# Attention and a gated feed-forward block on one core: contraction in pieces of 128 rows whose halves exchange column blocks, and a start on half of the first rows

## The chip, the cores and the metric

The kernel runs on one core of a Trainium2 chip. The metric is the device time of one execution in microseconds (us). Five engines run their own instruction streams and meet at semaphores: PE (TensorE; PEld is its weight load, which runs beside matmuls), DVE (VectorE), ACT (ScalarE), POOL (GpSimd) and SP (SyncE, which here only issues DMAs). PE writes its sums into PSUM, eight banks of 128 x 512 f32 numbers; ACT and DVE take them out into SBUF.

## What is computed

```python
xn = layernorm(x)                               # x: 2048 x 448, bf16
q  = (xn @ wq)                                  # 16 heads of 256
p  = softmax(q @ k.T * 256 ** -0.5)             # the last 512 cached keys; 8 key heads, each used by two
s  = concat(p @ v) @ wo
g  = silu((gelu(xn @ w_gate) * (xn @ w_up)) @ w_down)   # 1792 hidden columns
out = x + s * g
```

The contraction of the first products runs over D = 448 = 7 x 64 = 3 x 128 + 64 numbers. That remainder of 64 is what the change is about.

## The kernel before

A small recorder (`Rec.op`, L65) takes every operation in program order with the tiles that it reads and writes; each engine then executes its own list in that order, and the recorder derives the semaphore waits. So the order of the calls in the program is the order on each engine.

The 2048 rows are worked in NQC = 4 chunks of QC = 512 rows, each of TPC = 4 tiles of 128 rows.

**Start.** SP issues four DMAs for the tiles of chunk 0, then the gate and up weights in four slices (`load_gu`), chunk 1's rows after the second slice, then w_down and the other rows. PE spins on zeros (`warm(12)`, L308). DVE computes the statistics of the four tiles (`ln_stats`, L293), ACT the square roots for two tiles at a time (L335), DVE normalises (`ln_norm`, L299), PE transposes each tile in 14 pieces (`ln_tr`, L321), and ACT or DVE copies the 128 x 896 result into `xnT` (L327, L329).

**Layout.** `xnT` holds the transposed rows in NK = 7 pieces of 64, each stored twice: on partitions 0 to 63 and again on 64 to 127. The gate weights lie on partitions 0 to 63 and the up weights on 64 to 127 of one tile `wgu`; `wq` holds the even head of a pair below and the odd head above. A matmul of 64 rows uses half of PE, so two run side by side, a "pair": the lower half of the array makes the gate column block in one bank, the upper half the up block in the next.

**Feed-forward stage, `gate_up` (L367).** For each chunk, 14 blocks f of 7 pairs. Block n takes the banks 2(n mod 3) and the next one. ACT applies gelu to the gate bank (L379, 128x512), DVE multiplies the up bank by it (L381, 128x512) into `actT`. While this runs, `ln_later` and `ln_later2` prepare the next chunk: statistics on DVE, 1/std on POOL, two normalised copies on DVE (L299 twice), and a DMA transposition on SP's queue (L241) into `xnT`. After the 14 blocks come four `down` products (L387) for the chunk's tiles; those of the last chunk are spread over the attention's first slots (`fill`).

**Queries, `q_burst` (L407).** Four heads at once, later eight: per block 7 pairs into two banks (alternating 0-1 and 2-3; in the first burst 4-5, 0-1, 2-3, 0-1), and one ACT copy of 128x1024 (L422).

**Attention.** 64 heads-by-chunk, four slots of 128 rows each: `scores` (L433, banks 4 and 5 in turn, exponential on ACT L437, reciprocal and scaling on DVE L439 and L440, DMA transposition on SP), `values` (L453, copied out by DVE L459), and the output product `outproj` (L473). The last tiles end on DVE (L482, L484) and four output DMAs.

POOL's queue carries the wq, V and wo pieces (`load_piece`), one after each of certain blocks.

Of the kernel before, what the change touches and what calls it, by code (L numbers as in the profile page):

```python
# [22 lines left out]
class Rec:  # L23
# [41 lines left out]
    def op(self, eng, fn, r=(), w=(), dma=False, after=(), lane=None):  # L65
# [17 lines left out]
        for d, raw in deps:  # L83
            if d.eng == eng and not d.dma and not dma and (eng == "tensor" or not raw and eng != "gpsimd"):
                continue
            d.inc = d.waited = True
            o.deps.append(d)
# [54 lines left out]
def bass_recurrent_scan__sliding_block_cached__geglu_ffn__prompt_kernel(nc, A_x, A_k, A_v, A_wq, A_wo, B_x, B_wg, B_wu, B_wd, out):  # L142
# [6 lines left out]
    QC, TPC, HP = 512, 4, 64  # L149
    NQC = S // QC  # L150
    NT = NQC * TPC
    NK = D // HP
    NF, NJ, NE = F // P, W // P, Dh // P
    assert S % QC == 0 and D % HP == 0 and NE == 2 and NJ == 4 and Hq == 2 * Hkv and Hq % 4 == 0 and NF % 2 == 0
# [4 lines left out]
    with es:  # L159
# [20 lines left out]
        xnT, _ = sb("xnT", [P, NQC, NK, QC], BF16)  # L180
# [3 lines left out]
        wq, _ = sb("wq", [P, NK, Hkv, Dh], BF16)  # L184
        wo, _ = sb("wo", [P, Hq * NE, D], BF16)
        gu_at = off[0]
        wgu, x_at = sb("wgu", [P, NK, F], BF16)
        x4, _ = sb("x4", [P, NT, D], BF16)
        NX = 4
        xn2, d_at = sb("xn2", [P, NX, NK, 2, HP], BF16)  # L190
        wd, _ = sb("wd", [P, NF, D], BF16)
        actT, hb_at = sb("actT", [P, NF, QC], BF16)
        NHB = 4
        hb, ffn_end = sb("hb", [P, NHB, QC], BF16)

# [11 lines left out]
        def fill_pr(at, end):  # L207
            while at + 2 * W <= end:
                t_, at = sb("pr%d" % len(pr), [P, W], BF16, at)
                pr.append(t_)  # L210
# [33 lines left out]
        dve(lambda e: e.memset(actT[:, NF - 1, :], 0.0), w=[("actT", NF - 1)])  # L244
# [9 lines left out]
        wg_v = B_wg.rearrange("(k p) f -> p k f", p=HP)  # L254
        wu_v = B_wu.rearrange("(k p) f -> p k f", p=HP)
        cuts = [0, 2, 6, 10, NF]
        fslice = {f: s for s in range(4) for f in range(cuts[s], cuts[s + 1])}

        def load_gu(s):
            a, b = cuts[s] * P, cuts[s + 1] * P  # L260
            dma("sync", wgu[0:HP, :, a:b], wg_v[:, :, a:b], w=[("wgu", 0, s)])
            dma("sync", wgu[HP:P, :, a:b], wu_v[:, :, a:b], w=[("wgu", 1, s)])
# [5 lines left out]
        act(lambda e: e.activation(small[:, 2:3], small[:, 0:1], ACT.Sqrt), r=[("eps",)], w=[("warm",)])  # L268
        for sl in range(4):
            load_gu(sl)  # L270
            if sl == 1:
                load_x(1)
        dma("sync", wd[:, :, :], B_wd.rearrange("(f p) d -> p f d", p=P), w=[("wd",)])
        for c in range(2, NQC):
# [5 lines left out]
        wq_v = A_wq.rearrange("(k p) (g two m) -> p k g two m", p=HP, two=2, m=Dh)  # L280
        pieces = [(wq[lo * HP:(lo + 1) * HP, k, :, :], wq_v[:, k, :, lo, :], ("wq", lo, k))
                  for k in range(NK) for lo in range(2)]
# [13 lines left out]
        def ln_norm(t, copies=2):  # L296
            s = t % NX
            for o in range(copies):
                dve(lambda e, o=o: e.tensor_scalar(  # L299
                    xn2[:, s, :, o, :], x4[:, t, :].rearrange("p (k d) -> p k d", k=NK), mv[:, t, 0:1],  # L300
                    rstd[:, t:t + 1], op0=ALU.subtract, op1=ALU.mult),
                    r=[("x4", t), ("mv", t), ("rstd", t)], w=[("xn2", s, o)])

        def warm(n):

            def run(e):
                for _ in range(n):
                    ins = e.matmul(bank(3), lhsT=actT[:, NF - 1, 0:P], rhs=actT[:, NF - 1, :], start=True, stop=True)  # L308
                return ins
            pe(run, r=[("actT", NF - 1)], w=[("ps", 3)])  # L310

        def ln_tr(t):
            parts = ((act, 4),), ((dve, 5),), ((act, 6),), ((dve, 7),)
            parts = [(eng, b, 0, NK) for eng, b in parts[t]]
            for eng, b, a, z in parts:
                tp = bank(b).bitcast(BF16)

                def tr(e, tp=tp, a=a, z=z):
                    for k in range(a, z):
                        for lo in (0, HP):  # L320
                            ins = e.transpose(tp[lo:lo + HP, (k - a) * P:(k - a + 1) * P], xn2[:, t, k, 0, :], ident[:, :])  # L321
                    return ins
                pe(tr, r=[("xn2", t, 0), ("ident",)], w=[("ps", b)])
                dst = xnT[:, 0, a:z, t * P:(t + 1) * P]
                src = tp[:, 0:(z - a) * P].rearrange("p (k q) -> p k q", q=P)
                if eng is act:
                    act(lambda e, dst=dst, src=src: e.activation(dst, src, ACT.Copy), r=[("ps", b)], w=[("xnT", 0, t, a)])  # L327
                else:
                    dve(lambda e, dst=dst, src=src: e.tensor_copy(dst, src), r=[("ps", b)], w=[("xnT", 0, t, a)])  # L329

        for t in range(TPC):
            ln_stats(t)
            if t % 2:
                a, b = t - 1, t + 1
                act(lambda e, a=a, b=b: e.activation(std[:, a:b], mv[:, a:b, 1], ACT.Sqrt, bias=small[:, 0:1]),  # L335
                    r=[("mv", a), ("mv", t), ("eps",)], w=[("std", a)])
        for a in range(0, TPC, 2):
            dve(lambda e, a=a: e.reciprocal(rstd[:, a:a + 2], std[:, a:a + 2]),  # L338
                r=[("std", a)], w=[("rstd", a), ("rstd", a + 1)])
            ln_norm(a, 1)  # L340
            ln_norm(a + 1, 1)
        warm(12)
        for t in range(TPC):
            ln_tr(t)
        xn0 = [("xnT", 0, t, 0) for t in range(TPC)]
# [9 lines left out]
        def ln_later2(t):  # L355
            c, t4 = divmod(t, TPC)
            ln_norm(t)
            dmaT(xnT[:, c, :, t4 * P:(t4 + 1) * P], xn2[:, t % NX, :, :, :].rearrange("p k a d -> p (k a d)"),
                 r=[("xn2", t % NX, 0), ("xn2", t % NX, 1)], w=[("xnT", c, t4)])

        def xn(c):
            return [("xnT", c, t) for t in range(TPC)] if c else xn0
# [4 lines left out]
        def gate_up(c, f):  # L367

            n = c * NF + f
            s = 2 * (n % NGB)  # L370

            def run(e):
                for k in range(NK):
                    for b, lo in ((s, 0), (s + 1, HP)):
                        ins = e.matmul(bank(b), lhsT=wgu[lo:lo + HP, k, f * P:(f + 1) * P],  # L375
                                       rhs=xnT[lo:lo + HP, c, k, :], start=k == 0, stop=k == NK - 1)
                return ins
            pe(run, r=xn(c) + [("wgu", 0, fslice[f]), ("wgu", 1, fslice[f])], w=[("ps", s), ("ps", s + 1)])
            act(lambda e: e.activation(hb[:, n % NHB, :], bank(s), ACT.Gelu_apprx_tanh),  # L379
                r=[("ps", s)], w=[("hb", n % NHB)])  # L380
            dve(lambda e: e.tensor_tensor(actT[:, f, :], bank(s + 1), hb[:, n % NHB, :], ALU.mult),  # L381
                r=[("ps", s + 1), ("hb", n % NHB)], w=[("actT", f)])

        def down(c, t, part=range(NF)):
            b = (6, 7, 7, 2)[t] if c == NQC - 1 else 6 + t % 2
# [21 lines left out]
        def q_burst(i0, heads):  # L407

            c, h0 = divmod(i0, Hq)
            for n in range(heads):  # L410
                hp, e_ = divmod(n, 2)
                s = 2 * (n % 2) if i0 else (4, 0, 2, 0)[n]
                buf, name, _ = q_slot(i0 + 2 * hp)

                def run(e, hp=hp, e_=e_, s=s):
                    for k in range(NK):
                        for b, lo in ((s, 0), (s + 1, HP)):
                            ins = e.matmul(bank(b), lhsT=wq[lo:lo + HP, k, h0 // 2 + hp, e_ * P:(e_ + 1) * P],  # L418
                                           rhs=xnT[lo:lo + HP, c, k, :], start=k == 0, stop=k == NK - 1)
                    return ins  # L420
                pe(run, r=xn(c) + [("wq", lo, k) for lo in range(2) for k in range(NK)], w=[("ps", s), ("ps", s + 1)])
                act(lambda e, e_=e_, s=s, buf=buf: e.activation(  # L422
                    buf[:, :, e_, :], psum[:, s * 512:(s + 2) * 512].rearrange("p (a q) -> p a q", a=2), ACT.Copy),
                    r=[("ps", s), ("ps", s + 1)], w=[(name, e_)])
# [94 lines left out]
        for c in range(NQC):  # L519
            lead = 4 if c == 0 else 1  # L520
            for f in range(NF):
                gate_up(c, f)
                if c + 1 < NQC and lead <= f < lead + 2 * TPC:
                    t, half = divmod(f - lead, 2)
                    (ln_later2 if half else ln_later)((c + 1) * TPC + t)
# [15 lines left out]
        for d, slots in ((0, range(0, 4)), (1, range(4, 12)), (2, range(16, 20)), (3, range(20, 24))):  # L541
# [4 lines left out]
        for i in range(NI):  # L546
            for t in range(TPC):
                scores(i, t)
                if 4 * i + t in fill:
# [53 lines left out]
```

## Time and profile before

| | us |
|---|---|
| median of 3 runs (558.99 to 559.34) | 559.27 |
| the execution that the profile shows | 558.75 |
| its span, first to last instruction | 557.0 |
| PE busy in the span | 548.7 |
| DVE, ACT, POOL busy | 324.1, 296.3, 89.7 |
| first `gate_up` matmul starts at | 9.28 |
| `gate_up`, one chunk (196 matmuls) | 21.3 |
| `down`, one chunk (56 matmuls) | 10.7 |
| `q_burst` of four heads, of eight | 6.0, 12.2 |

Times inside the execution are counted from the span's start. In a timeline line the first number is the start, the second the time from the group's first start to its last end, then engine, line of the kernel, operation, what it writes and reads, shape and count; in brackets stands the engine's idle time before it and what ended it. A matmul's shown duration includes its passage through the array, so consecutive ones overlap: the rate is read from start to start.

### The profile page before, as it was taken

What the parts mean: (1) busy time and instruction counts of PE and PEld (TensorE: products, weight loads), DVE (VectorE), ACT (ScalarE), POOL (GpSimd) and SP (SyncE); (2) the same over time, 40 slices, a digit from 0 to 9 for tenths busy, and PEclk for the clock granted to TensorE, in tenths of its full rate; (3) what the DMA queues carried; (4) which work ended last, traced back from release to release, by engine and by line L of the source; (5) the groups of instructions that cost most, each with busy time, mean ns of one, the idle gap of its engine ahead of it and who ended that gap; (6) DMA issues with size and microseconds to landing.
All of it is one profiled execution on the core that took longest, in us unless ns stands there. A gap on an engine that the chain in (4) does not pass through costs nothing.

```text
span 557.0 us, 9857 instructions
## 1 busy us (share of the span) xinstructions
PE 548.7 (99%) x3498; PEld 258.8 (46%) x3532; DVE 324.1 (58%) x835; ACT 296.3 (53%) x673; POOL 89.7 (16%) x125
## 2 busy tenths in 40 slices
PE   8999999999999999999999999999999999999997
PEld 4544444444444444444444444444444444444445
DVE  5727446143462688078728744782688078638774
ACT  4423233247746665655575656556665655565631
POOL 0232323200000121001411110042121002411123
PEclk9999999999999999999999999999999999999999
DMA  8996846932453365245535542445354254634552
GB/s 196 276 177 102 138 102 143 264 110 70 95 87 67 67 96 98 46 94 104 112 81 95 104 86 44 100 92 137 75 96 100 34 95 97 120 88 98 93 95 52
DMA packets 169552, 58.83 MB, mean 106 GB/s; under 512 B 160160, under 2 KB 166432, under 8 KB 169504
## 3 DMA queue, kind: packets, MB, share of 16 engines
q1 hardware_dynamic: 166208, 45.50, 44.3%
q0 software_dynamic: 3152, 12.65, 8.7%
q8 instruction: 28, 0.46, 0.4%
q14 instruction: 20, 0.16, 0.1%
q10 hardware_dynamic: 144, 0.06, 0.0%
HBM read 17.92 MB, written 1.84 MB: 35 GB/s over the span
## 4 chain that ended last, share of the span: by engine, by line
PE 97%; DVE 2%; issue 1%; DMA 0%; ACT 0%
PE ps L453 20%; PE ps L433 20%; PE ps L418 18%; PE ps L473 17%; PE ps L375 15%; PE ps L387 8%; DVE tmp L482 0%; DVE xr L484 0%; DVE stats L293 0%; DMA x<-in_A_x_dram 0%; PE ps L321 0%; ACT xnT L327 0%; DVE mv L294 0%; DVE xn L299 0%; DVE rstd L338 0%
## 5 line engine op out<-in xcount | busy, mean ns | idle before, releaser
L437 ACT ACTIVATE pr<-ps 128x512 bf16<-128x512 f32 x256 | 152.7, 597 | 121.4 <-PE ps L433 117.9
L433 PE MATMUL ps<-kT,qT 128*128 128x512 bf16 x493 | 147.7, 379 | 2.0 <-issue 1.4
L453 PE MATMUL ps<-pT,V 128*128 128x512 bf16 x497 | 129.1, 379 | 0.8
L439 DVE RECIPROCAL rden<-den 128x1 f32<-128x1 f32 x256 | 41.5, 162 | 148.2 <-ACT pr L437 129.8
L473 PE MATMUL ps<-wo,oT 128*128 128x448 bf16 (+1 forms) x536 | 116.2, 344 | 0.0
L440 DVE TENSOR_SCALAR pr<-pr,rden 128x512 bf16<-128x512 bf16 x256 | 108.0, 422 | 9.0
L418 PE MATMUL ps<-xnT,wq 64*128 64x512 bf16 x896 | 98.3, 376 | 0.0
L422 ACT ACTIVATE qT<-ps 128x1024 bf16<-128x1024 f32 x64 | 65.5, 1023 | 40.6 <-PE ps L418 40.6
L375 PE MATMUL ps<-xnT,wgu 64*128 64x512 bf16 x784 | 85.3, 376 | 0.8 <-ACT xnT L327 0.8
L459 DVE CAST oT<-ps 128x512 bf16<-128x512 f32 x124 | 84.5, 682 | 0.7 <-PE ps L453 0.5
L453 PEld LDWEIGHTS ps<-pT,V 128*128 128x128 bf16 x512 | 50.0, 98 | 60.2 <-issue 0.3
L473 PEld LDWEIGHTS ps<-wo,oT 128*128 128x128 bf16 x536 | 52.4, 98 | 51.0
L433 PEld LDWEIGHTS ps<-kT,qT 128*128 128x128 bf16 x512 | 49.1, 98 | 55.8 <-issue 4.5
L381 DVE TENSOR_TENSOR actT<-ps,hb 128x512 bf16<-128x512 f32 x56 | 38.1, 685 | 57.2 <-ACT hb L379 55.3
L418 PEld LDWEIGHTS ps<-xnT,wq 64*128 64x128 bf16 x896 | 43.0, 94 | 54.6 <-DVE acc L494 2.5
L379 ACT ACTIVATE hb<-ps 128x512 bf16<-128x512 f32 x56 | 33.4, 597 | 51.4 <-PE ps L375 51.4
L375 PEld LDWEIGHTS ps<-xnT,wgu 64*128 64x128 bf16 x784 | 39.4, 94 | 46.0 <-issue 1.6
L437 ACT ACTIVATION_READ_ACCUMULATOR pr<-ps 128x1 f32 x256 | 49.8, 195 | 0.0
L387 PE MATMUL ps<-wd,actT 128*128 128x448 bf16 x224 | 46.2, 353 | 0.1
L498 POOL TENSOR_TENSOR tmp<-acc,gy 128x448 f32<-128x448 f32 x16 | 16.5, 1034 | 158.6 <-DVE acc L494 158.6
L513 POOL TENSOR_SCALAR tmp<-tmp 128x448 f32<-128x448 f32 x16 | 9.0, 563 | 187.8 <-ACT tmp L512 187.8
L387 PEld LDWEIGHTS ps<-wd,actT 128*128 128x128 bf16 x224 | 21.7, 98 | 22.2 <-issue 1.3
(43 smaller groups left out, 172.4 us busy)
## 6 DMA issues: line engine op xcount, KB each, us to landing
pT<-pr SPq DMA_TRANSPOSE x256, 2.4
wq<-in_A_wq_dram POOLq DMA_DIRECT2D x14, 256.0 KB, 5.2
wo<-in_A_wo_dram POOLq DMA_DIRECT2D x4, 896.0 KB, 6.6
V<-in_A_v_cache_dram POOLq DMA_DIRECT2D x4, 512.0 KB, 5.0
xr<-in_A_x_dram POOLq DMA_DIRECT2D x4, 448.0 KB, 3.9
wd<-in_B_w_down_dram SPq DMA_DIRECT2D x1, 1568.0 KB, 18.5
wgu<-in_B_w_gate_dram SPq DMA_DIRECT2D x3, 448.0 KB, 9.5
wgu<-in_B_w_up_dram SPq DMA_DIRECT2D x3, 448.0 KB, 11.1
```

Of the source, the lines that this page charges most:

```text
L375: ins = e.matmul(bank(b), lhsT=wgu[lo:lo + HP, k, f * P:(f + 1) * P], rhs=xnT[lo:lo + HP, c, k, :], start=k == 0, stop=k == NK - 1)
L381: dve(lambda e: e.tensor_tensor(actT[:, f, :], bank(s + 1), hb[:, n % NHB, :], ALU.mult), r=[("ps", s + 1), ("hb", n % NHB)], w=[("actT", f)])
L387: pe(lambda e, f=f: e.matmul(bank(b, D), lhsT=actT[:, f, t * P:(t + 1) * P], rhs=wd[:, f, :], start=f == 0, stop=f == NF - 1), r=[("actT", ...
L418: ins = e.matmul(bank(b), lhsT=wq[lo:lo + HP, k, h0 // 2 + hp, e_ * P:(e_ + 1) * P], rhs=xnT[lo:lo + HP, c, k, :], start=k == 0, stop=k == ...
L422: act(lambda e, e_=e_, s=s, buf=buf: e.activation(buf[:, :, e_, :], psum[:, s * 512:(s + 2) * 512].rearrange("p (a q) -> p a q", a=2), ACT ...
L433: ins = e.matmul(bank(b), lhsT=buf[:, a, k, t * P:(t + 1) * P], rhs=kT[:, g, k, :], start=k == 0, stop=k == NE - 1)
L437: act(lambda e: e.activation(pr[s][:, :], bank(b), ACT.Exp, scale=scale, accum_out=den[:, s:s + 1]), r=[("ps", b)], w=[("pr%d" % s,), ("de ...
L439: dve(lambda e: e.reciprocal(rden[:, s:s + 1], den[:, s:s + 1]), r=[("den", s)], w=[("rden", s)])
L440: dve(lambda e: e.tensor_scalar(pr[s][:, :], pr[s][:, :], rden[:, s:s + 1], None, op0=ALU.mult), r=[("pr%d" % s,), ("rden", s)], w=[("pr%d ...
L453: ins = e.matmul(bank(b), lhsT=V[:, j, g, e_ * P:(e_ + 1) * P], rhs=pT[:, i % NPT, j, :], start=j == 0, stop=j == NJ - 1)
L459: dve(lambda e: e.tensor_copy(dst, bank(b)), r=[("ps", b)], w=[key])
L473: ins = e.matmul(bank(b, D)[:, lo:hi], lhsT=oT[G % 2][:, idx, t * P:(t + 1) * P], rhs=wo[:, h0 * NE + idx, lo:hi], start=idx == 0, stop=id ...
```

## The change

The contraction is cut into KF = 3 pieces of 128 and one of 64. `xnT` now holds each of the three pieces once, over all 128 partitions, and only the last 64 rows twice. Gate and up weights become separate tiles `wg` and `wu` of 128 partitions, and their last 64 rows lie in `wg6` and `wu6`: even column blocks on partitions 0 to 63, odd ones on 64 to 127. The same is done to `wq` (`wq6`).

A block now makes two neighbouring column blocks of one matrix, m = 0 and 1, in two phases. In phase 0 the lower half of the array works for m = 0 and the upper half for m = 1 on the three pieces and the last one (4 pairs). In phase 1 the halves exchange: the lower half adds its rows to m = 1 and the upper half to m = 0 (3 pairs). Phase 1 waits by semaphore for phase 0 of the same block (`hard`), and the next block's phase 0 is put between them.

So a `gate_up` block is either two gate column blocks or two up column blocks: gelu and the multiplication each run on 128x1024, half as often. `hb` has two buffers of that size. `q_burst` goes round three bank pairs, 0-1, 2-3 and 4-5.

At the start the square roots are taken tile by tile; tiles 0 and 1 are transposed and copied first, and the first three blocks run on their 256 rows with the transpositions of tiles 2 and 3 put in behind the third block's phase 0 and the second block's phase 1; then the same three blocks run on the other 256 rows. `warm` runs 38 and 4 matmuls of 128 columns. The first pieces of `wg6` and `wu6` are loaded by ACT's queue, the rest by SP's behind chunk 1's rows. `ln_later2` makes one normalised copy on DVE and a 128x64 copy on ACT. The `fill` of the last chunk's `down` for tiles 2 and 3 moves four slots forward and within a slot behind `values` and `q_burst`; the first part stands ahead of the first `scores`. `pr` has 12 buffers, where 10 found room before.

```diff
+        def two_blocks(ph, c, s, cols, w, w6, keys, q0=0, q1=QC):
+            def run(e):
+                for k in range(KF + 1 - ph):
+                    for lo in (0, HP):
+                        m = (lo > 0) ^ ph
+                        lhsT = w[lo:lo + HP, k, cols[m]:cols[m] + P] if k < KF else w6[lo:lo + HP, :]
+                        ins = e.matmul(bank(s + m)[:, q0:q1], lhsT=lhsT, rhs=xnT[lo:lo + HP, c, k, q0:q1],
+                                       start=ph == 0 and k == 0, stop=ph == 1 and k == KF - 1)
+                return ins
+            hard = [phase0[s]] if ph else []
+            phase0[s] = pe(run, r=xn(c)[q0 // P:q1 // P] + keys, w=[("ps", s), ("ps", s + 1)], hard=hard)
...
-        def gate_up(c, f):
+        def gate_up(c, f, ph, q0=0, q1=QC):
+            j, up = divmod(f, 2)
             n = c * NF + f
-            s = 2 * (n % NGB)
+            s, h = 2 * (n % NGB), (n // 2) % NHB
...
+            two_blocks(ph, c, s, (2 * j * P, (2 * j + 1) * P), w, w6[:, j, :], keys, q0, q1)
+            if ph == 0 or q1 < QC:
+                return
+            two = psum[:, s * 512:(s + 2) * 512].rearrange("p (a q) -> p a q", a=2)
+            if up:
+                dve(lambda e: e.tensor_tensor(actT[:, 2 * j:2 * j + 2, :], two, hb[:, h, :, :], ALU.mult),
+                    r=[("ps", s), ("ps", s + 1), ("hb", h)], w=[("actT", 2 * j), ("actT", 2 * j + 1)])
+            else:
+                act(lambda e: e.activation(hb[:, h, :, :], two, ACT.Gelu_apprx_tanh),
+                    r=[("ps", s), ("ps", s + 1)], w=[("hb", h)])
...
         def q_burst(i0, heads):
-                s = 2 * (n % 2) if i0 else (4, 0, 2, 0)[n]
+                s, h = 2 * ((n + (0 if i0 else 2)) % 3), h0 + 2 * hp
...
+            for n in range(heads + 1):
+                if n < heads:
+                    part(n, 0)
+                if n:
+                    part(n - 1, 1)
...
         def ln_later2(t):
             c, t4 = divmod(t, TPC)
             ln_norm(t)
+            act(lambda e: e.activation(xn2[:, t % NX, D:D + HP], xn2[:, t % NX, D - HP:D], ACT.Copy),
+                r=[("xn2", t % NX, 0)], w=[("xn2", t % NX, D)])
...
+        warm(38)
+        for t in range(2):
+            ln_stats(t)
+            ln_std(t)
+        load_gu6(w_gu[1:], 0, 2, "scalar")
+        for t in range(2):
+            ln_first(t)
+            ln_tr(t)
+        warm(4)
+        ln_copy(0)
+        ln_stats(2)
+        ln_copy(1)
+        ln_std(2)
+        ln_stats(3)
+        ln_std(3)
+        act(lambda e: e.activation(small[:, 3:4], small[:, 0:1], ACT.Gelu_apprx_tanh), r=[("eps",)], w=[("warm2",)])
+        for t in range(2, TPC):
+            ln_first(t)
...
         for c in range(NQC):
-            lead = 4 if c == 0 else 1
-            for f in range(NF):
-                gate_up(c, f)
+            lead = 6 if c == 0 else 2
+            done = 0
+            if c == 0:
+                done = NGB
+                for f in range(NGB + 1):
+                    if f < NGB:
+                        gate_up(0, f, 0, 0, QC // 2)
+                    if f:
+                        if f > 1:
+                            ln_tr(f)
+                            ln_copy(f)
+                        gate_up(0, f - 1, 1, 0, QC // 2)
+            for f in range(NF + 1):
+                if f < NF:
+                    gate_up(c, f, 0, QC // 2 if f < done else 0)
+                if f:
+                    gate_up(c, f - 1, 1, QC // 2 if f - 1 < done else 0)
+                t = (f - lead) // 2
+                if c + 1 < NQC and t >= 0 and f % 2 == 0:
+                    if 1 <= t <= TPC:
+                        ln_later2((c + 1) * TPC + t - 1)
+                    if t < TPC:
+                        ln_later((c + 1) * TPC + t)
...
-        for d, slots in ((0, range(0, 4)), (1, range(4, 12)), (2, range(16, 20)), (3, range(20, 24))):
+        for d, slots in ((0, range(0, 4)), (1, range(4, 12)), (2, range(12, 16)), (3, range(16, 20))):
...
+                if i + t == 0:
+                    down(NQC - 1, *fill[0])
                 scores(i, t)
-                if 4 * i + t in fill:
-                    down(NQC - 1, *fill[4 * i + t])
...
+                if i + t and 4 * i + t in fill:
+                    down(NQC - 1, *fill[4 * i + t])
```

The transposition `ln_tr(t)` of a tile is now three 128 x 128 pieces and the last 64 columns twice, into bank 6 or 7; `ln_copy(t)` copies 128x512 (ACT for tiles 0 and 2, DVE for 1 and 3). Weight slices are cut at column-block pairs 0, 1, 2, 4, 7, so each slice of `wg` or `wu` is 128 partitions x 3 x 256, 256, 512 and 768 columns; the remainder pieces are 64 partitions x 2 or 5 runs of 128 columns (256 bytes each).

## The prediction

> **What bounds the kernel now.** First the page's busy times and its chain of work: PE works 99% of the span and 97% of the chain is PE. Then the busy times by stage, to see where PE is not full.
>
> ```profile
> PE 548.7 (99%) x3498; PEld 258.8 (46%) x3532; DVE 324.1 (58%) x835; ACT 296.3 (53%) x673; POOL 89.7 (16%) x125
> ...
> PE 97%; DVE 2%; issue 1%; DMA 0%; ACT 0%
> ```
> ```profile
> 0.00:9.28 9.28, 6.95 (x69) 3.35 (x70) 6.27 (x17) 4.12 (x7) 0.73 (x8) 1.00 0.77 171
> 9.28:126.47 117.19, 117.19 (x954) 55.76 (x956) 55.31 (x103) 40.43 (x68) 26.38 (x46) 1.00 0.80 166
> 126.47:133.00 6.53, 6.37 (x59) 2.84 (x56) 0.69 (x1) 5.48 (x7) 0.56 (x1) 1.00 0.25 75
> 133.00:549.30 416.30, 413.65 (x2377) 192.55 (x2408) 256.47 (x701) 246.32 (x593) 62.03 (x70) 1.00 0.47 88
> ```
>
> The columns are the stretch, its length, then busy time and count of PE, PEld, DVE, ACT and POOL, and PE's granted clock. From 9.28 us to 126.47 PE is never idle, and over the attention it lacks 2.65 us of 416. Only the 9.28 us ahead of the first gate_up matmul, spent on spinning and transposing, can be shortened. The change keeps the number of half-row pairs, 7 per block, so the rest can only stay as it is or get holes.
>
> The timeline gives the prices.
>
> ```profile
> 9.28 15.07 PE L375 MATMUL ps<-xnT,wgu 64*128 64x512 bf16 x138 [0.77 <-ACT xnT L327]
> 11.00 0.60 ACT L379 ACTIVATE hb<-ps 128x512 bf16<-128x512 f32 x1 [0.65 <-PE ps L375]
> 11.71 0.69 DVE L381 TENSOR_TENSOR actT<-ps,hb 128x512 bf16<-128x512 f32 x1 [2.53 <-ACT hb L379]
> ...
> 12.51 0.60 ACT L379 ACTIVATE hb<-ps 128x512 bf16<-128x512 f32 x1 [0.91 <-PE ps L375]
> ```
> ```profile
> L422 ACT ACTIVATE qT<-ps 128x1024 bf16<-128x1024 f32 x64 | 65.5, 1023 | 40.6 <-PE ps L418 40.6
> L381 DVE TENSOR_TENSOR actT<-ps,hb 128x512 bf16<-128x512 f32 x56 | 38.1, 685 | 57.2 <-ACT hb L379 55.3 <-PE ps L387 1.6
> L299 DVE TENSOR_SCALAR xn<-x,mv,rstd 128x448 bf16<-128x448 bf16 x28 | 12.9, 501 | 5.2 <-POOL rstd L352 5.1
> L482 DVE TENSOR_TENSOR tmp<-ps,gy 128x224 f32<-128x224 f32 x6 | 2.3, 383 | 0.0
> ```
> ```profile
> 140.20 0.19 ACT L437 ACTIVATION_READ_ACCUMULATOR pr<-ps 128x1 f32 x1
> 140.45 0.16 PEld L433 LDWEIGHTS ps<-kT,qT 128*128 128x128 bf16 x2 [0.24 <-ACT pr L437]
> 140.51 0.59 PE L433 MATMUL ps<-kT,qT 128*128 128x512 bf16 x2
> ```
>
> The gelus follow each other by 1.51, so a block of 7 pairs takes 1.51, a pair 0.216, phase 0 0.86, phase 1 0.65; half a phase 0 (256 columns) 0.43, half a phase 1 0.32. Block 0 ends at 9.28+1.51 = 10.79 and its gelu starts at 11.00: **0.21** from a block's end to its eviction. ACT ends at 140.39, the matmul that waited starts at 140.51: **0.12** from release to matmul.
>
> **Part 1, the start.** DVE's statistics of tiles 0 and 1 stay at 2.81 to 4.38. ACT now issues two DMAs ahead of its first square root; at 0.37 each (ACT's issue of an output DMA at 554.25 in the timeline) they pass in 2.8 to 3.6, before the statistics are ready. Reciprocal and normalisation (0.17, then 0.50) end at 5.0 and 5.6, transposition of tile 1 at about 6.1, DVE's copy behind tile 2's statistics at 6.65 (128x896 took 0.62, the 512 columns 0.42). First gate_up matmul: **6.8** instead of 9.28. Spinning is 42 x 128 columns instead of 12 x 512, less in columns, and is over by then.
>
> I compare the point at which blocks 0 to 2 and block 3's phase 0 are done: 25 pairs, before at 9.28+25x0.216 = 14.67. After: gate half-phase 6.8 to 7.23; the first up slice landed at 3.37+4.1 = 7.47; it now ends with the 768th run of 512 bytes instead of the 896th, but small pieces run beside it: 7.5, so 7.93; phase 1 to 8.25; block 2 needs the second gate slice, between landings at 7.47 (0.46 MB) and 9.73 (0.92 MB) by bytes about 8.4: to 8.83. Tile 2's transposition 0.25 with 0.10 of change of array shape on both sides (values at 143.37, four by 0.216, should hand over at 144.23 and the half-row matmul starts at 144.33), phase 1, tile 3 likewise: 9.95; copy 0.2+0.42, restart 0.12: second halves from 10.7. Block 0 ends at 11.9, its gelu frees the bank at 11.9+0.21+1.02+0.12 = 13.25, while PE is there at 12.66: **0.59 idle**; block 3's phase 0 to 14.1, phase 1 of block 2 to 14.4; block 4 waits for block 1's multiplication, which waited for that gelu: 14.6, where 14.67 stood. So the 2.5 us won are given back: 0.9 in transpositions among the blocks, 0.7 for evictions that come too soon after each other, 0.9 in weights and copies. I take **0.0**. Bounds: with no wait for weights or copies 6.8+5.4+0.9+0.7 = 13.8, a gain of 0.8. On the other side the late pieces. By the landings of single DMAs a 448 KB slice on 64 partitions took 2.3 us (200 GB/s), w_down on 128 partitions 4.5 us for 1568 KB (357 GB/s), the first slice, of short runs, 2.0 us for 224 KB (115 GB/s). Counted from 7.5, the rest of wg6 is the end of 1.34 MB and of chunk 1's rows (1.2 us): at 270 GB/s it lands at 13.7, and is needed at 14.6. At 200, and 115 for the short runs, it lands at 16.0, 1.4 late; with a restart the bound is a loss of 1.5. I take the middle rate, as the new slices have 128 partitions like w_down but shorter runs.
>
> [...] No row here shows a load of 256-byte runs. [...]
>
> **Part 2, gate_up steady.** Phase 1's self-wait looks back 1.51 us (phase 1 and phase 0 of the neighbours lie between): nothing. A block's banks are wanted by the third block on, 1.51 after its end. Gelu on 1024 columns, at the price of L422 (L379 and L437 both take 597 for 512): 0.21+1.02+0.12 = 1.35: hidden, with 0.16 to spare. The multiplication: (685-383)/288 = 1.05 ns a column, so 1024 cost 1.22: 0.21+1.22+0.12 = **1.55, 0.04 too late**. Before, 128x512 had 3 us. It bites at f = 1, 3, 5, 7, 9 of four chunks: 20 x 0.035 = **0.7**. Then the 128x64 copy on ACT (0.22, on the line through 0.60 for 128x512 and 1.02 for 128x1024; 128x1 takes 0.20). It waits for DVE's normalisation, which waits behind the up multiplication, and the next gelu is queued behind it. Chain from the up block's end: 0.21+1.14+0.50+0.03+0.22+1.02+0.12, less 0.07 overlap on ACT, is 3.17 against two blocks, 3.06; it can bite at 11 places (3, 4 and 4 in chunks 0 to 2), a delay at one giving air to the next: at most 0.12 each, nothing if the contiguous copy runs at L440's 0.35. I take **0.4**. Together **1.1**, bounds 0 (release runs ahead as the 0.08 overlap between DVE's instructions does) and 2.6 (0.10 restart at every multiplication). The normalisation made once instead of twice saves DVE 0.4, and transposing 4 blocks instead of 7 saves DMA time; both are off the path. The last transposition of chunk 1 is issued some 1.6 later (f = 14 instead of 11): before 31.2, landing 8.6 after, wanted at 41.3; now 41.4 at the old latency, less for the smaller tile: 0, at most 1. POOL's 22 weight pieces keep count and place.
>
> **Part 3, leaving the first q_burst.**
>
> ```profile
> 132.44 0.11 PEld L433 LDWEIGHTS ps<-kT,qT 128*128 128x128 bf16 x2 [0.42 <-issue]
> 132.56 1.02 ACT L422 ACTIVATE qT<-ps 128x1024 bf16<-128x1024 f32 x1 [0.49 <-PE ps L418]
> 132.68 0.38 PE L433 MATMUL ps<-kT,qT 128*128 128x512 bf16 x1 [0.16 <-issue]
> ```
>
> Now scores start while ACT still copies the last block, since that lies in banks 0-1. In the new rotation (4, 0, 2, 4) the last block lies in banks 4-5, which the first scores need, and the last two blocks end only 0.65 apart, so their copies queue on ACT: the second ends 1.54 after the burst, PE may go on at 1.65. Ahead of scores stand three down matmuls, 3x0.19, and the 0.10 of shape: 0.67. Idle **1.0**; bounds 0.7 (a single copy) and 1.1. Later bursts end in banks 0-1 and 2-3: their exponentials start 0.3 later, but the bank is wanted 2.6 after the burst and free at 2.3: 0. The moved down parts: PE work, only reordered; slots 20 to 23 then go at the 0.86 of slots 24 to 27, above ACT's 0.79 (0.60+0.19): 0. The tail is untouched.
>
> **Sum.** 0.0+1.1+1.0 = 2.1 on 558.75: 560.9 for an execution like the profiled one. The median of the runs stands 0.52 above that execution, so **561.4**. Bounds summed: -0.8+0+0.7 = -0.1, and 1.5+2.6+1.1 = 5.2 (the late transposition could add 1; not all come at once).
>
> **Rivals.** (A, forecast, 0.50) holes as counted: 560.4 to 562.8. (B, 0.24) "nothing left": the evictions just fit and the start gains its 0.8 while the burst costs 0.7 to 1.0: 559.2 to 560.4. For it: slack of 0.04 is within what a start-to-start reading gives. (C, 0.18) weights or the last transposed tile late: in the page's slices the DMA engines are 80 to 90% busy over the first 40 us, and before, the second up slice landed at 12.0 for a use at 12.3: 562.8 to 565. (D, other side, 0.08) the head start arrives whole: 2.5 less 0.9 for the transpositions, 1.6, all holes hidden: 557.7. It decides if block 3's first matmul is issued before 12.7 and the first scores without a hole; against it, block 0's gelu cannot start before its second half. That the exchange breaks the side-by-side running would cost 0.216 per pair, over a hundred us; the two halves still write two banks, and I give it nothing of its own.
>
> A difference of 0.2% (1.1 us) is about what a measurement here can tell from no change: slower 0.68 (A and C), same 0.24, faster 0.08. The range 558.9 to 564.6 takes in A, B and most of C.
>
> **What would show it.** First gate_up matmul near 6.8 and block 4 near 14.6; idle of about 0.6 before block 3, released by ACT's gelu; PE waiting on DVE's 1024-wide product by some 0.03 twenty times; a 1.0 hole before the first scores, released by ACT's copy. Wrong if products take under 1.18, if PE waits for weights after 14 us, or if PE's holes lie in the attention.

## The result, and the profile after

The changed kernel takes **564.15 us** (median of 5 runs, 563.90 to 565.56) beside 559.07 us for the kernel before (5 runs, 558.95 to 559.34): ratio 1.0097, with a 95% interval of 1.0082 to 1.0112. It is slower by 5.1 us, where the sum of the forecast gave 2.1 over the profiled execution, 2.3 over this median. The profiled execution took 564.13 us, its span is 562.3 us (before 557.0).

From the page of the changed kernel, PE's busy time and two rows of the 40 slices:

```profile
PE 551.2 (98%) x3534; PEld 260.4 (46%) x3568; DVE 313.9 (56%) x797; ACT 292.0 (52%) x660; POOL 88.2 (16%) x125
...
PE   7999999999999999999999999999999999999997
...
PEclk8999999999999999999999999999999999999999
```

PE's busy time grew by 2.5 us although the products are the same, and the clock's row, all nines before, begins with an 8: the same work took longer at a lower granted clock (0.66 from 10.10 to 17.90, below). Both lie in the first slice of 14 us, so the stretches there are read one by one (columns as in the prediction):

```profile
0.00:7.00 7.00, 5.56 (x53) 4.80 (x54) 3.98 (x13) 2.86 (x6) 0.74 (x8) 1.00 0.66 168
7.00:10.10 3.10, 0.61 (x8) 0.35 (x9) 1.32 (x6) 1.78 (x3) 0.00 (x0) 0.77 1.07 329
10.10:17.90 7.80, 7.44 (x82) 4.90 (x83) 0.42 (x1) 1.62 (x2) 0.00 (x0) 0.66 1.11 308
17.90:35.08 17.18, 17.18 (x160) 7.21 (x161) 10.93 (x16) 5.89 (x9) 3.68 (x8) 1.00 0.51 157
35.08:131.00 95.92, 95.92 (x760) 43.25 (x760) 34.39 (x48) 29.68 (x43) 21.11 (x38) 1.00 0.61 131
```

PE does 0.61 us of work between 7.00 and 10.10, then 7.8 us at a mean granted clock of 0.66; from 17.9 it is never idle until the first q_burst. The timeline of PE names what it waited for, and ACT's and SP's queues say when that was issued:

```profile
7.00 0.61 PE L410 MATMUL ps<-xnT,wg 64*128 64x256 bf16 x8 [0.46 <-DMA wg<-in_B_w_gate_dram]
10.11 1.04 PE L410 MATMUL ps<-xnT,wu 64*128 64x256 bf16 x8 [2.50 <-DMA wu<-in_B_w_up_dram]
...
17.89 0.39 PE L410 MATMUL ps<-xnT,wu 64*128 64x512 bf16 x2 [0.35 <-ACT hb L434]
```
```profile
4.40 0.60 ACTq L246 DMA_DIRECT2D wu<-in_B_w_up_dram  x1
...
5.04 0.62 ACTq L246 DMA_DIRECT2D wu<-in_B_w_up_dram  x1
```

The first up half-phase (phase 0 of the first up block, on 256 rows) had its slice of `wu` by 7.06 us, but it also multiplies the last 64 rows, `wu6`, whose two first pieces ACT's queue issued behind the first square root, at 4.40 and 5.04. They landed at 8.40 and 9.97. The same eight matmuls that take 0.61 us at 7.00 take 1.04 at 10.11: the clock fell to half at 8.64 us and came back at 15.47.

The stages, from their first matmuls, add up:

| | before | after | grows by |
|---|---|---|---|
| chunk 0's `gate_up` over at | 30.54 | 35.08 | 4.55 |
| `gate_up` of chunks 1, 2, 3 | 21.26, 21.26, 21.16 | 21.26, 21.26, 21.16 | 0 |
| first to second q_burst | 18.02 | 18.98 | 0.96 |
| second to third q_burst | 25.63 | 25.37 | -0.26 |
| third burst to the end of the span | 387.00 | 387.12 | 0.12 |

(Differences are taken before rounding; what lies between these rows, `down` and the bursts, is the same.) The 0.96 is the predicted hole, released by ACT's copy out of the last burst block:

```profile
138.76 0.81 PE L488 MATMUL ps<-kT,qT 128*128 128x512 bf16 x3 [1.02 <-ACT qT L471]
```

### The profile page after: what moved, and what is told of

It reads as the page before. It is cut to its first block, busy times and chain, and to the rows that moved or that the text cites. A ratio compares the mean times of both kernels' runs of the same rounds, so it can differ in the third digit from the quotient of the medians.

```text
span 562.3 us, 9800 instructions
## 1 busy us (share of the span) xinstructions
PE 551.2 (98%) x3534; PEld 260.4 (46%) x3568; DVE 313.9 (56%) x797; ACT 292.0 (52%) x660; POOL 88.2 (16%) x125
## 4 chain that ended last, share of the span: by engine, by line
PE 73%; DVE 1%; issue 1%; DVEq 0%
PE ps L508 20%; PE ps L488 19%; PE ps L528 16%; PE ps L410 16%; PE ps L440 2%; DVE tmp L537 0%; DVE xr L539 0%; DVEq L128 0%
## 5 line engine op out<-in xcount | busy, mean ns | idle before, releaser
L431 DVE TENSOR_TENSOR actT<-ps,hb 128x1024 bf16<-128x1024 f32 x28 | 34.3, 1225 | 70.6 <-PE ps L410 63.1
L410 PE MATMUL ps<-xnT,wu 64*128 64x512 bf16 (+1 forms) x406 | 48.8, 373 | 2.8 <-DMA wu<-in_B_w_up_dram 2.5
L410 PE MATMUL ps<-xnT,wg 64*128 64x512 bf16 (+1 forms) x420 | 49.3, 369 | 0.5 <-DMA wg<-in_B_w_gate_dram 0.5
L434 ACT ACTIVATE hb<-ps 128x1024 bf16<-128x1024 f32 x28 | 28.5, 1017 | 33.9 <-PE ps L410 33.9
```

Of the source, the lines that this page charges most:

```text
L410: ins = e.matmul(bank(s + m)[:, q0:q1], lhsT=lhsT, rhs=xnT[lo:lo + HP, c, k, q0:q1], start=ph == 0 and k == 0, stop=ph == 1 and k == KF - 1)
L431: dve(lambda e: e.tensor_tensor(actT[:, 2 * j:2 * j + 2, :], two, hb[:, h, :, :], ALU.mult), r=[("ps", s), ("ps", s + 1), ("hb", h)], w=[( ...
L434: act(lambda e: e.activation(hb[:, h, :, :], two, ACT.Gelu_apprx_tanh), r=[("ps", s), ("ps", s + 1)], w=[("hb", h)])
```

## Experiments

The theory after the result: the loss is (1) the late `wu6` pieces, (2) half clock that the hole brings on, (3) the exit of the first q_burst; the new layout and the double-width evictions cost nothing. Rivals: the layout itself slows the first chunk; pieces in runs of 256 bytes are slow wherever they stand; the head start is worth its 2.5 us, and something else takes it away. Ratios are against runs of the kernel before that stood beside them: 558.92 us (13 runs) for the wu6 piece alone, the spins, the eight `down` matmuls and both edits; 558.79 (17) for the order of the loads, the early pieces and the two first kernels without a head start; 559.03 (23, from 558.64 to 564.31) for the last three.

**The late piece.** The first pieces of `wu6` go on SP's queue, right behind the first up slice.

```diff
+            if sl == 0:
+                load_gu6(w_gu[1:], 0, 2, "sync")
...
-        load_gu6(w_gu[1:], 0, 2, "scalar")
```

> The changed kernel with one edit: the first remainder pieces of the up weights go on SP's queue right behind the first up slice, not on ACT's queue behind the square roots. Theory (this piece alone makes the 2.5 us hole at 7.6, and the hole makes PE's clock fall to half from 8.6 to 15.5): the piece lands by about 8, the hole shrinks below 0.7, the clock stays full, chunk 0 ends 3.5 to 4.5 earlier, total 559.6 to 560.7. Rival 1 (the weights as a whole come too late): the hole moves to the next slice, at most 1 us won, total above 563. Rival 2 (half clock comes from the small matmuls and transpositions, not from the hole): the hole goes, the clock still falls, total about 561.5.

Measured: 561.46 us, ratio 1.0042 (1.0026 to 1.0059), so 2.7 us better than the change, but above the forecast of 559.6 to 560.7. The pieces landed at 6.78 and 7.33, and the 2.5 us hole is gone. The profiled run, at 563.62 the slowest of four (the others 560.89 to 561.77), has another one:

```profile
17.02 1.04 PE L411 MATMUL ps<-xnT,wg 64*128 64x512 bf16 x8 [2.38 <-DMA wg<-in_B_w_gate_dram]
```

That is the rest of `wg6`, behind chunk 1's rows on SP's queue: now that PE comes 4 us earlier it is the next one late, at 16.48 and 16.89 in this run. (In the change it was issued 1.3 us earlier and landed at 13.97 and 14.42, when PE wanted it only after 18.) The clock fell again after that hole (18.0 to 21.4). One late piece had covered for another.

**The clock alone.** The hole stays, but PE spins in it.

```diff
                 for f in range(NGB + 1):
+                    if f == 1:
+                        warm(44)
                     if f < NGB:
```

> The changed kernel with 44 spinning matmuls of 128 columns put between the first gate half-block and the first up half-block, on PE alone; the piece still lands at about 10. Theory: the wait stays, but PE is busy in it, so the clock stays full after it; from 10.1 the 17 half pairs and the transpositions run in half the time, and the second halves start about 2 us earlier (13.3 instead of 15.4); total 562.0 to 562.5. Rival 2 (clock falls for another reason): no change, 564.1. If the wait alone counted and half clock cost nothing: 564.1 with a full clock.

Measured: 562.81 us, ratio 1.0075 (1.0060 to 1.0090), a little above the forecast. The hole is filled, and the half clock is gone:

```profile
7.75 2.63 PE L328 MATMUL ps<-actT 128*128 128x128 bf16 x44
10.31 0.61 PE L410 MATMUL ps<-xnT,wu 64*128 64x256 bf16 x8
```

The up half starts no earlier than in the change (10.31 against 10.11; the piece was there at 9.87, the spins ran on past it), but takes 0.61 again, and the first chunk is over at 33.33 instead of 35.08. From the start of the up half to the end of the chunk that is 23.01 instead of 24.98: the half clock alone cost **1.97 us** in the profile. Less the 0.21 of the later start that is 1.75; the medians differ by 1.3 (four runs here, from 562.36 to 564.40).

**The exit of the first burst.** Eight `down` matmuls ahead of the first scores instead of three, taken from the next slots.

```diff
+        for s, a, z in ((0, 0, 8), (1, 8, 10), (2, 10, 12), (3, 12, 14)):
+            fill[s] = 0, range(a, z)
```

> The changed kernel with 8 instead of 3 down matmuls of the last chunk's first tile ahead of the first scores, 2 each in slots 1 to 3. Theory (the 1.02 us hole ahead of the first scores is ACT's queue of two copies out of banks 4-5, and can be filled): hole under 0.1, total 563.1 to 563.3. Rival (the hole is only moved, since ACT's exponentials then bind in slots 1 to 3): the hole comes back there, 563.9 or more.

Measured: 563.66 us, ratio 1.0083 (1.0068 to 1.0098); by the medians 0.5 us less than the change, which the scatter hardly carries, where 0.85 to 1.05 were forecast. The profile is clearer: no wait ahead of the scores, and first to second burst 18.26 instead of 18.98. The covering work fills 0.72 of the 0.96; 0.24 stays, without any idle time that the trace lists.

**Both.** The first and the third edit together.

> The first and third edits together. Theory: the two add up, total 558.6 to 559.7, that is the kernel before or a little better. If the edits hide each other: above 560.2.

Measured: 560.05 us over ten runs from 558.93 to 561.07, ratio 1.0018 (1.0008 to 1.0027), just above the forecast of 558.6 to 559.7. In its profiled run, the fastest, the rest of `wg6` was issued at the same times as in the first experiment (7.89 and 8.54) and landed at 14.27 and 14.60 instead of 16.48 and 16.89: no hole, first chunk over at 30.60. The same landing lies 2 us apart in these two profiles, which fits a spread of 2 us; the other runs have no profile.

**The order of the loads.** Beside both edits, the rests of `wg6` and `wu6` go ahead of the third slices and of chunk 1's rows.

```diff
+            if sl == 1:
+                load_gu6(w_gu, 2, NF2, "sync")
             if sl == 2:
                 load_x(1)
-                load_gu6(w_gu, 2, NF2, "sync")
```

> The changed kernel with two things put right: the order of the loads on SP's queue (the first pieces of wu6 right behind the first up slice instead of on ACT's queue; the rests of wg6 and wu6 behind the second slices instead of behind the third), and eight down matmuls ahead of the first scores instead of six. The computation is unchanged. Theory (the changed kernel's loss over the kernel before is nothing but late small pieces, with the half clock that the hole they leave brings on, and the exit of the first q_burst): no hole over 0.5 us anywhere in the first chunk, the clock at 1.0 from 5.5 us on, first gate_up at 6.9 to 7.2, first chunk over at 30.4 to 30.8 (before 30.53), no hole ahead of the first scores, the whole within 0.2% of the kernel before and with less spread than the run that moved wu6 alone: 558.5 to 560.0. Rival (the small pieces on SP's queue only move the lateness on to the slices behind them): a hole of 1 to 2.5 us at the second or third slice, first chunk over at 32 or later, 560.5 to 562.

Measured: **558.97 us** in eleven runs from 558.68 to 559.12, ratio 0.9999 (0.9990 to 1.0008). The spread is gone with the late pieces, and the whole loss with it; no cost of the layout is left. Its PE timeline shows what a head start with everything in time looks like:

```profile
6.80 0.61 PE L412 MATMUL ps<-xnT,wg 64*128 64x256 bf16 x8 [0.26 <-ACT std L357]
7.60 0.61 PE L412 MATMUL ps<-xnT,wu 64*128 64x256 bf16 x8 [0.19 <-DMA wu<-in_B_w_up_dram]
...
10.92 0.61 PE L412 MATMUL ps<-xnT,wg 64*128 64x256 bf16 x8 [0.18 <-DVE xnT L352]
...
13.41 1.04 PE L412 MATMUL ps<-xnT,wu 64*128 64x512 bf16 x8 [0.35 <-ACT hb L436]
```

First matmul 2.48 us earlier than before, first chunk over at 30.61, 0.07 later than before. From start to start against the steady rate (0.108 a pair of 256 columns) the two transpositions and the changes of array shape cost 1.13, the up half's weights 0.37, tile 3's copy 0.36, the gelu that block 3's banks wait for 0.54.

**Early, on ACT's queue.** All four first pieces are issued on ACT's queue at the start, without waiting for x.

```diff
-        load_gu6(w_gu[:1], 0, 2, "scalar", after=x0[:1])
+        load_gu6(w_gu, 0, 2, "scalar")
...
-        load_gu6(w_gu[1:], 0, 2, "scalar")
```

> The changed kernel, with the first pieces of wg6 and wu6 all issued at the start on ACT's queue, one behind the other, waiting neither for the first rows of x nor for the statistics. The computation is unchanged. It asks why the first wu6 pieces came at 8.39 and 9.97 us. Theory A (they were issued too late, at 4.39 and 5.03 us, when the second slices were being moved): issued by 4 us they land by 7.5, the 2.50 us hole is gone or under 0.7, the clock holds 1.0, and the whole is 559.5 to 562. Theory B (four pieces in short runs on ACT's queue are slow wherever they stand): they still land at 8.5 or later, the hole stays 1.5 us or more, the clock still falls, and the whole is 563 to 565. A price either way: the first rows of x, which they no longer wait for, may land up to 0.5 us later and the first gate_up with them.

Measured: 560.77 us, ratio 1.0032 (1.0020 to 1.0043). Issued at 2.26 and 2.92, the `wu6` pieces landed at 4.89 and 5.64. The lists of DMA issues, in the change and here (count, KB each, median us from issue to landing):

```profile
wu<-in_B_w_up_dram ACTq DMA_DIRECT2D x2, 32.0 KB, 4.5
```
```profile
wu<-in_B_w_up_dram ACTq DMA_DIRECT2D x2, 32.0 KB, 2.7
```

Same queue, same runs of 256 bytes, 1.8 us less on the way: they were late since they were issued 2 us later, behind the first slices and the second gate slice; from 4.4 to 8.4 us the DMA engines were 0.99 busy. Place and time were moved together here, so how much each is worth stays open. The rival falls. What this kernel still loses to the kernel before is the burst's exit (0.96) and a first chunk over at 31.07, with a first `gate_up` at 7.22.

**No head start.** All four tiles first, then full blocks; the rest of the change stays. Once with the change's three `down` matmuls ahead of the scores, once with eight.

```diff
-            b = 6 + t % 2
+            b = 4 + t
...
-        for t in range(2):
+        for t in range(2, TPC):
+            ln_stats(t)
+            ln_std(t)
+        for t in range(TPC):
             ln_first(t)
             ln_tr(t)
...
-            if c == 0:
-                done = NGB
-                for f in range(NGB + 1):
...
```

> The changed kernel without its head start: all four row tiles are normalised and transposed first (into four banks), and the first three blocks of gate_up run on all 512 rows from the beginning, as the other blocks do; everything else of the change stays, the first pieces of wu6 on ACT's queue and the six down matmuls included. The computation is unchanged. Theory (the new layout costs nothing in gate_up, and the loss is the head start running into pieces that land at 8.4 to 10 us): first gate_up at 8.6 to 9.3, its gate half takes longer than a half-row block (1.5 us), so that the up block waits 0.2 to 1.0 us, no half clock, first chunk over at 30.3 to 31.3, the 1.02 us hole ahead of the first scores remains, the whole 559.0 to 560.8. Rival (the layout itself, 64-partition loads and double-width evictions, costs the first chunk its 4.5 us): the first chunk is over at 34 or later and the whole is 563 or more.

> The kernel without the head start, and with eight down matmuls ahead of the first scores instead of six. The computation is unchanged. Theory: 1.0 us less than the same without the eight matmuls, so 558.0 to 559.8, and the 1.02 us hole ahead of the first scores gone. Rival (the hole only moves behind the moved matmuls): same time as without them within 0.3 us.

(These two expectations and that of the order put right speak of six matmuls ahead in the change; it has three.) Measured: 561.76 us, ratio 1.0043 (1.0028 to 1.0058), and 562.17, ratio 1.0054 (1.0041 to 1.0066): the forecasts are missed by 1.0 and by 2.4 us. The spins had been cut for a start on two tiles and ran out. PE's waits in the first of the two, whose clock is half from 7.53 to 14.36, begin with that:

```profile
PE ps L338 <- DVE xn L320: 1.5, 1, 1.5
PE ps L328 <- DVE actT L252: 1.0, 1, 1.0
PE ps L486 <- ACT qT L469: 0.8, 1, 0.8
PE ps L408 <- ACT xnT L351: 0.6, 1, 0.6
```

In the second (a wait of 1.2 us for the first tiles, half clock from 9.04 to 12.45) the 0.8 us at the scores is gone, but a wait of 0.73 for the scaled probabilities takes its place later in that stage. Why there is open; the next kernel, the same in that stage, does not have it.

**No head start, with its disturbances taken out.** Ten spins more ahead of the transpositions, six behind them, and SP's order as put right above.

> No head start again, with its two disturbances taken out: ten more spin matmuls ahead of the transposes and six behind them, so that the clock has no idle stretch to fall in, and the first pieces of wu6 and the two rests on SP's queue as in the kernel with the order put right; eight down matmuls ahead of the first scores. Only extra spins are computed beside the work. Against the kernel with the order put right it differs in the head start alone. Theory (with the pieces in time, the head start gives back by its own waits and transposes what it gains at the start, so it is worth nothing): first gate_up at 9.0 to 9.5, clock 1.0 throughout, first chunk over at 30.3 to 30.8, whole 558.6 to 559.5. Rival 1 (the head start is worth its 2.5 us, and the new layout costs 2.5 us elsewhere in the first chunk): first chunk over at 32 or later, whole 560.5 to 562. Rival 2 (the clock still falls): as without the spins, 561 to 562.5.

Measured: 558.83 us (12 runs), ratio 0.9989 (0.9973 to 1.0005); first `gate_up` at 9.14, first chunk over at 30.40, full clock over this stretch. From 9.13 on PE is as full as before, with the new layout:

```profile
9.13:30.40 21.27, 21.26 (x197) 10.40 (x197) 10.94 (x16) 8.06 (x12) 3.68 (x8) 1.00 0.96 271
```

It differs from the kernel with the order put right (558.97) in the head start and its spins alone: as the change builds it, the head start is worth nothing that can be measured.

**Its own waits taken away.** Block 3 goes into the banks of the transpositions, tiles 2 and 3 are transposed a half-row block earlier.

```diff
+            if c == 0 and f >= NGB:
+                s = 6 if f == NGB else 2 * ((n - 1) % NGB)
...
+                    if f in (1, 2):
+                        ln_tr(f + 1)
+                        ln_copy(f + 1)
                     if f:
-                        if f > 1:
-                            ln_tr(f)
-                            ln_copy(f)
                         gate_up(0, f - 1, 1, 0, QC // 2)
```

> The kernel with the order of loads put right and eight down matmuls ahead, and beside that the head start's own two waits taken away: the fourth block goes into the two banks that the transposes leave free instead of the pair that the first gelu still has to read, and tiles 2 and 3 are transposed one half-row block earlier, both copied out by VectorE. The computation is unchanged. Theory (these two waits, 0.54 and 0.36 us over the steady distance of blocks, lie on the path of TensorE and nothing else is late behind them): the first chunk is over at 29.6 to 29.9 instead of 30.61, and the whole is 557.9 to 558.5, faster than the kernel before by 0.3 to 0.9 us. Rival (the slices of the weights, which land at 13.2 and 14.3 us for the fifth and sixth blocks, are next in line): a new wait of 0.3 to 0.9 us at the third slice, first chunk over at 30.2 or later, whole 558.6 to 559.1 or more, with a wider spread.

Measured: **558.44 us** (12 runs, 558.05 to 559.13), ratio 0.9981 (0.9963 to 0.9998): faster than both kernels, though by less than 0.2%: 0.6 us under the runs of the kernel before beside it, which scatter, and 0.35 to 0.5 under its other two medians. The head start's part of the span, from first matmul to the end of chunk 0, has no idle time left, although it starts at 7.37 instead of 6.80 (`wg6`'s second piece landed at 7.24):

```profile
0.00:7.37 7.37, 5.58 (x52) 4.78 (x53) 4.23 (x14) 2.85 (x6) 0.73 (x8) 1.00 0.62 157
7.37:29.80 22.43, 22.43 (x248) 11.74 (x249) 12.84 (x23) 8.70 (x13) 3.67 (x8) 1.00 0.89 273
```

**Room in the steady blocks.** One more VectorE instruction ahead of every up product.

```diff
             if up:
+                dve(lambda e: e.tensor_copy(probe[:, n:n + 1], psum[:, s * 512:s * 512 + 1]), r=[("ps", s)], w=[("probe", n)])
```

> The changed kernel with one more VectorE instruction, a one-column copy out of PSUM, ahead of each of the 28 up products: it lengthens what VectorE does for each pair of blocks by 0.1 to 0.2 us. The result is unchanged. It asks how much room the double-width product has in gate_up. Theory (none: release, 1.225 us product and weight load fill the 1.51 us between two blocks exactly): from the second chunk on each of the seven up products of a chunk comes late by the length of the copy, so a gate_up stage takes 22.0 to 22.6 us instead of 21.26, and the whole is 2 to 4 us longer than the changed kernel. Rival (there is room, as the bank pairs are three): 21.26 us as before, the whole the same within 0.6 us.

Measured: 565.27 us in one run. Neither forecast of the time holds, but the theory of no room nearly does. The copy takes 0.16 but overlaps the product's start, which moves by 0.075; the product then ends 0.065 later, and the products follow each other by 3.075 instead of 3.022. So 0.053 of 0.065 is felt: the room is about 0.01 us. Each of the three stages takes 0.27 more than in the change (21.53, 21.52, 21.43), as five places a chunk would give.

## Why the prediction was right in sign and wrong in size

The sign held, and so did the burst's exit. One step of the first part failed, and it carries more than the missing 3 us: 4.55 came where 0.0 stood, while the 1.1 of the steady stages did not come. That the total is no further off is luck, two errors of opposite sign.

**The start: 0.0 taken, 4.55 measured.** The step that failed is "it now ends with the 768th run of 512 bytes instead of the 896th, but small pieces run beside it: 7.5". The slice was there at 7.06. The small pieces did not run beside it: they were issued 1.3 and 2.0 us after it from another queue, behind the second gate slice, and came at 8.40 and 9.97. The prediction had timed ACT's issue of the `wg6` pieces and never that of `wu6`. All issues behind ACT's first square root should have been put on the same clock as SP's, and at ACT's own price: an issue took 0.60 to 0.71 us there, not the 0.37 read from an output DMA, and held the first square root until 4.20, though its statistics were there at 3.63. Besides, the working put no price on an idle PE other than its own length: the second part of the bill was the clock. Against the kernel with the order put right, the up half starts 2.51 us later (10.11 instead of 7.60; that holds 0.2 for a first matmul at 7.00 instead of 6.80, since `wg6`'s second piece landed at 6.86), and from there the chunk takes 1.97 longer (24.98 instead of 23.01; with the hole spun full it is 23.01 too). With the 0.07 that this kernel itself lies behind the kernel before, that is all of the 4.55.

With the pieces in time the rest of that working stands: block 4 was predicted at 14.6 and starts there in the kernel with the order put right (13.41 plus 0.87 for the half-phase plus 0.33); the gain given back was put down as 0.9 transpositions, 0.7 evictions, 0.9 weights and copies, and is 1.13, 0.54 and 0.73. That they cancel to 0.0 so well is in part luck: each is off by about 0.2, one up and two down. The bound on the other side was real as well: the rest of `wg6`, predicted at 13.7 or, at the worse rate, 16.0 for a need at 14.6, landed at 13.97 and 14.42 in the change, and between 14.3 and 16.9 in the two kernels in which it was issued 1.3 us later and PE was early enough to want it.

**Steady `gate_up`: 1.1 taken, 0 measured.** The group of products confirms 1.22 us; the price of the release was wrong.

```profile
61.97 1.23 DVE L431 TENSOR_TENSOR actT<-ps,hb 128x1024 bf16<-128x1024 f32 x1 [0.74 <-PE ps L410]
62.63 1.68 PE L410 MATMUL ps<-xnT,wg 64*128 64x512 bf16 x14
63.11 0.39 DVE L320 TENSOR_SCALAR xn<-x,mv,rstd 128x448 bf16<-128x448 bf16 x1
63.25 0.56 PEld L410 LDWEIGHTS ps<-xnT,wg 64*128 64x128 bf16 x8 [0.30 <-DVE actT L431]
```

The product ends at 63.20; the weight load that waited for it starts 0.05 later and the matmul 0.03 after that, in step. So release costs 0.08 and not the 0.12 read at the scores, where a 128-row weight load stands in between: 0.21+1.225+0.08 = 1.515 beside the block's own length of 1.511. It is the engine's weight load that waits, PE itself does not. It fits by a hair: the probe shows a room of about 0.01. ACT's 128x64 copy took 0.26 (0.22 taken), but the normalisation 0.39 instead of 0.50, so that chain fits too.

**The burst's exit: 1.0 taken, 0.96 measured** by the hole that was described. **The moved fill: 0 taken, -0.26 measured**: in the second burst's stage PE stands idle for 0.16, 0.06 and 0.05 us before, and for 0.05 twice after; that is 0.17 of it, the other 0.09 is in no idle time. Whether the moved fill or the third bank pair takes it away was not tried. **The tail: 0 taken, 0.12 measured.**

Of the rivals, C (weights late) is what came, at 562.8 to 565, by pieces it did not name: it spoke of slices and of the last pieces after 14 us.

## What to carry to other kernels

When a head start moves the first consumer forward, list every transfer it needs with its queue, its issue time and what the queue's engine does ahead of it; a 32 KB piece issued at 4.4 us decided over 448 KB that were in time. When one piece is put right, the next in line shows: settle the order of all of them by time of need, and look at the spread of the runs for the ones that still come late. In the change a hole of 2.50 us in PE's first microseconds cost its length and, by the half clock that stood beside it, 1.97 us more; with 44 spins in it the clock stayed at 1.00. A wait that can't be avoided there can be spent spinning.

## What the runs showed of the hardware

**Half clock stood beside PE's holes.** Times at which the profiles show a granted clock of 0.50, and PE's wait near them:

| kernel | PE's wait, us | clock 0.50 |
|---|---|---|
| the change | 2.50, until 10.11 | 8.64 to 15.47 |
| eight `down` matmuls ahead | 2.7, for `wu` | 8.16 to 14.99 |
| the late piece moved alone | 2.38, until 17.02 | 18.01 to 21.43 |
| no head start | 1.5, for the first tiles | 7.53 to 14.36 |
| no head start, eight ahead | 1.2, for the first tiles | 9.04 to 12.45 |
| the hole filled with 44 spins | 0.7, until 7.21 | none (1.00) |

In the change (the stretch, its length, PE's busy time and count, PE's granted clock, then DMA share and GB/s):

```profile
8.64:15.47 6.83, 5.37 (x46) 0.50 1.11 296
15.47:17.90 2.43, 2.08 (x40) 1.00 1.07 355
```

Not every wait had half clock beside it: the 1.02 us ahead of the change's first scores (138.76) and the 0.77 ahead of the first `gate_up` matmul of the kernel before (9.28) stand at 1.00. What decides is not shown.

**The first spins ran at half speed.** The record of the granted clock begins at 5.23 us in the change and at 5.65 in the kernel before; ahead of that the rows show 1.00, but the spins tell otherwise: the change's first 38, of 128 columns, come 0.107 us apart, the 44 in the filled hole 0.056; the twelve of the kernel before, of 512 columns, come 0.427 apart, where 512 columns take 0.216 later.

```profile
0.98 4.24 PE L328 MATMUL ps<-actT 128*128 128x128 bf16 x38 [0.98 <-DVE actT L252]
```

**Short runs moved fewer bytes a ns.** In the change's trace of the first 20 us the middle run of 256 bytes took 18 ns, on ACT's queue as on SP's, the middle run of 512 bytes 27: 14 bytes a ns against 19. What made the pieces late was when, and behind what, they were issued: the same `wu6` pieces on the same queue took 4.5 us (median) from issue to landing when issued at 4.40 and 5.04, and 2.7 when issued at 2.26 and 2.92.

**Landings scatter.** The rest of `wg6`, same place and same issue times to 0.01 us, landed at 14.27 in the profiled run of the kernel with both edits and at 16.48 in that with the late piece moved alone. The ten runs of the first spread over 2.1 us; the eleven of the kernel with the order put right, where this transfer lands at 9.45 and 9.72, over 0.44. That late landings make the spread is the likely reading; no profile of the slower runs shows it.
